# Token mixtures as scaling and addition, two more kinds of work given a choice of engine, and a first unit in halves

## The chip, the cores and the metric

The kernel runs on one core of one Trainium2 chip. Its metric is the device time of one execution in microseconds. Three runs of the kernel before gave 168.01 (median), 167.43 and 169.7 us. A core has a matrix engine (PE; its weight loads are shown apart, as PEld), a vector engine (DVE), a scalar engine (ACT), a general engine (POOL) and a queue that issues most transfers (SP). Each of them runs its own list of instructions strictly in order and waits on semaphores for the others.

## The reference, cut to what matters

Attention over a window of 128 tokens plus the first 4 tokens of the sequence, for 4 sequences of 768 tokens, 8 heads of 64 columns; then, on the 512 columns that the heads give together, a feed-forward part whose inputs are mixed from each token and the one before it.

```python
keep = is_sink | in_window            # 4 first tokens, or 0 <= pos_q - pos_k < 128
scores = np.where(keep, scale * q @ k.T, -1e9)
a = softmax(scores)
x = heads_side_by_side(a @ v)         # (4, 768, 512)

x_prev = concat([zeros, x[:, :-1]])
xk = mu_k * x + (1.0 - mu_k) * x_prev
xr = mu_r * x + (1.0 - mu_r) * x_prev
k = np.maximum(xk @ w_k, 0.0)         # 512 -> 1024
v = k * k @ w_v                       # 1024 -> 512
r = 1.0 / (1.0 + np.exp(-(xr @ w_r)))
out = r * v
```

## The kernel before, in words

**Units.** The 3072 tokens are 12 units of 256 (three to a sequence). A unit u goes through four stages: `prepare` (casts of k, q, v from float32 to bf16 into kb, qb, vb, and transposes of kb and qb into kt and qt, by PE and a copy, or by a transposing transfer), `attend` (per pair of heads: scores into two PSUM banks, exponential on ACT into e, multiplication of e by a mask on DVE, product with the values, reciprocal of the sums, and x, the scaled result), `mix` (transpose of x into xt, where a column is a token; td = xt minus xt shifted by one token; xk and xr) and `ffn` (keys: xk times wk into PSUM; rl = max(0, keys); kk = rl squared; gate: xr times wr, then th = tanh; product: kk times wv; ob = (th + 1) times product; store).

**The mixtures.** mu x + (1 - mu) x_prev is computed as td mu + x_prev. Line 973 does both steps in one DVE instruction (scalar_tensor_tensor), on 256 tokens of one of four groups of 128 columns: eight instructions in a unit, 96 in all.

**Squares and values.** The square (L1047) is a DVE multiplication of rl by itself, 48 times, 512 columns each. The scaling of the attention result (L911) is a DVE multiplication of a PSUM bank by the reciprocal, 48 times, 256 columns each.

**Choice and order.** Every operation is recorded with its engine (`P.op`), what it reads and writes, and the buffers that it takes from and holds in pools. Some have alternatives (`alts`); the table `CHOICE` says by number which one is built: the relu (L1035 on ACT, L1039 on DVE), the casts (L648 to L655, L714), the copies out of PSUM (L695, L700, L944), the casts of the weights (L609 to L615). `ORDER` holds a list of operations for each engine, written out by hand or by a search ahead of time; the planner walks these lists with assumed costs, only to give every operation its buffer and to place a few warming matmuls (L1098, L1101) in PE's early gaps. What runs on an engine, and in which order, is thus fixed by the two tables. A list that is late somewhere holds up all that stands behind it.

**The first unit.** Its k and q are loaded in two halves by heads (L455): heads 0 to 3 of all 256 tokens, then heads 4 to 7. Its keys need xk of all four groups of columns and all 256 tokens.

**Transfers.** All loads, the transposing transfers (L669, L955) and the stores (L1090, L1010) are issued by SP, except two small loads of mu by ACT. The weights come in five pieces of 1 MB (L473): two of wk, one of wr, two of wv. Outputs leave from ob, which has three buffers. The last 128 tokens are stored in two parts (L1010), of 128 and 384 columns, both by SP.

Of the kernel before, what the change touches and what calls it, by code (L numbers as in the profile page):

```python
# [18 lines left out]
    79: "POOL", 80: "POOL", 81: "POOL", 84: "ACT", 87: "ACT", 89: "DVE", 92: "DVE",  # L19
    94: "DVE", 95: "DVE", 97: "DVE", 98: "DVE", 131: "DVE", 134: "POOL", 137: "POOL",  # L20
    140: "ACT", 141: "DVE", 159: "PE/full", 171: "PE/tiles", 182: "POOL", 185: "POOL",
    187: "DVE", 191: "DVE", 195: "DVE", 241: "PE/tiles", 253: "PE/full", 264: "POOL",
    270: "POOL", 273: "DVE", 276: "ACT", 289: "DVE", 345: "POOL", 348: "POOL", 351:
    "DVE", 354: "POOL", 357: "ACT", 404: "PE/full", 416: "PE/tiles", 429: "POOL", 432:
    "POOL", 434: "POOL", 437: "DVE", 438: "ACT", 447: "DVE", 484: "PE/tiles", 496:
    "PE/full", 514: "POOL", 517: "ACT", 586: "POOL", 588: "POOL", 591: "POOL", 596:
    "ACT", 643: "PE/tiles", 655: "PE/full", 666: "POOL", 668: "POOL", 675: "ACT", 721:
    "PE/tiles", 733: "PE/tiles", 744: "POOL", 746: "POOL", 748: "POOL", 752: "ACT",
    753: "ACT", 819: "POOL", 821: "POOL", 823: "POOL", 828: "DVE", 847: "DVE", 872:
    "PE/tiles", 884: "PE/full", 897: "POOL", 901: "POOL", 904: "ACT", 923: "DVE", 948:  # L30
    "PE/tiles", 960: "PE/full", 979: "DVE", 1015: "DVE", 1019: "DVE",
# [19 lines left out]

OCT = range(1, 12)
# [282 lines left out]
def kernel(  # L335
# [14 lines left out]
    nc = tc.nc  # L350
# [807 lines left out]
```

## Time and profile before

| what | value |
|---|---|
| three runs, median (lowest, highest) | 168.01 us (167.43, 169.7) |
| the profiled execution's own time | 168.08 us |
| its span in the profile | 166.4 us |
| granted TensorE clock | 0.997 |
| PE busy | 155.0 us, 93% |
| DVE busy | 149.9 us, 90% |
| ACT busy | 116.6 us, 70% |
| POOL busy | 35.4 us, 21% |
| transfers | 34.38 MB, packets take 88.0% of the 16 engines' span |

The span runs from the first to the last instruction of the profiled execution; the execution's own time is 1.68 us longer. Busy time is a union: where instructions overlap, or the next begins before the end of the one before is recorded, nothing is counted twice. An instruction's duration is therefore longer than the distance at which a row of the same instructions starts; for sums on a full engine the distance from start to start counts, and that is what the chain of work and the timeline give. A PE that is busy in the profile may still wait a little between two matmuls, since their ends are modelled.

### The profile page before, as it was taken

The numbers are of one execution on the slowest core, as the hardware profiler recorded it, in microseconds if no ns is written. First come the engines' busy times: TensorE is split into PE (matmuls) and PEld (weight loads), VectorE is DVE, ScalarE is ACT, GpSimd is POOL, SyncE is SP. The second block draws the span as 40 slices with busy tenths as digits, with TensorE's granted clock in tenths as the row PEclk, the third lists the DMA queues.
The fourth block names the chain that finished last, engine by engine and source line by source line (L and its number), as shares of the span: only waits on it lengthen the run. The fifth ranks groups of instructions, "written<-read, shape, count | busy, mean of one in ns | idle before, by whom it ended". The sixth has DMA issues, their size and how long they took to land.

```text
span 166.4 us, 4712 instructions
## 1 busy us (share of the span) xinstructions
PE 155.0 (93%) x1858; PEld 102.4 (62%) x1858; DVE 149.9 (90%) x385; ACT 116.6 (70%) x190; POOL 35.4 (21%) x68
## 2 busy tenths in 40 slices
PE   7978678999999999999999999999998999999992
PEld 3545455665668586667567786485654664767541
DVE  7479999999899999999999999999979989995931
ACT  3388957996799999997978997783781647244111
POOL 2983332003606022134030060210210100000000
PEclk9999999999999999999999999999999999999998
DMA  4999999999898999999799999998995973301033
GB/s 133 253 373 389 241 260 328 387 360 325 198 290 230 229 246 248 195 226 197 173 234 138 161 206 197 219 207 109 209 174 113 246 199 126 121 9 63 0 132 120
DMA packets 74453, 34.38 MB, mean 207 GB/s; under 512 B 63800, under 2 KB 66112, under 8 KB 74432
## 3 DMA queue, kind: packets, MB, share of 16 engines
q1 hardware_dynamic: 74416, 34.09, 88.0%
q8 instruction: 14, 0.23, 0.6%
q14 instruction: 7, 0.06, 0.1%
q10 hardware_dynamic: 16, 0.00, 0.0%
HBM read 24.12 MB, written 6.29 MB: 183 GB/s over the span
## 4 chain that ended last, share of the span: by engine, by line
PE 35%; DVE 32%; DMA 16%; SPq 9%; issue 3%; POOL 2%; DVEq 0%; POOLq 0%
PE bank L1074 12%; DMA ks<-in_k_dram 11%; PE bank L1025 10%; DVE e L875 6%; DVE xr L973 5%; PE bank L1056 5%; SPq L431 5%; DVE x L911 4%; DVE xk L973 4%; DVE ob L1083 4%; DVE kk L1047 3%; DVE td L962 3%; DMA xt<-x 3%; DMA out_dram<-ob 3%; PE bank L681 2%
## 5 line engine op out<-in xcount | busy, mean ns | idle before, releaser
L1025 PE MATMUL bank<-xk,wk_sb 128*128 128x256 bf16 x384 | 50.9, 273 | 1.7 <-ACT rl L1035 1.0
L861 ACT ACTIVATE e<-sc 128x1024 bf16<-128x1024 f32 (+1 forms) x48 | 45.0, 966 | 4.9 <-PE sc L789 4.7
L1074 PE MATMUL bank<-wv_h,kk 128*128 128x512 bf16 x184 | 46.5, 379 | 1.4 <-DVE ob L1083 1.4
L1025 PEld LDWEIGHTS <-wk_sb 128*128 128x128 bf16 x384 | 35.6, 98 | 11.2 <-DVE wk_sb L615 1.3
L1035 ACT ACTIVATE rl<-bank 128x512 bf16<-128x512 f32 x44 | 25.8, 612 | 14.5 <-PE bank L1025 9.7
L875 DVE TENSOR_TENSOR e<-e,mask 128x1024 bf16<-128x1024 bf16 (+1 forms) x48 | 30.7, 654 | 0.3 <-ACT e L861 0.3
L1074 PEld LDWEIGHTS <-kk 128*128 128x128 bf16 x184 | 16.8, 97 | 16.3 <-issue 2.2
L1056 PE MATMUL bank<-wr_sb,xr 128*128 128x512 bf16 x96 | 24.5, 379 | 0.1
L973 DVE SCALAR_TENSOR_TENSOR xr<-td,mu_all,xt 128x256 bf16<-128x256 bf16 x48 | 24.4, 516 | 0.0
L1062 ACT ACTIVATE th<-bank 128x512 f32<-128x512 f32 x24 | 14.5, 609 | 10.9 <-PE bank L1056 9.6
L973 DVE SCALAR_TENSOR_TENSOR xk<-td,mu_all,xt 128x256 bf16<-128x256 bf16 x48 | 21.7, 479 | 0.1
L1047 DVE TENSOR_TENSOR kk<-rl 128x512 bf16<-128x512 bf16 x48 | 19.5, 425 | 0.3 <-ACT rl L1035 0.3
L911 DVE TENSOR_TENSOR x<-bank,rec 128x256 bf16<-128x256 f32 x48 | 19.4, 414 | 0.2
L1083 DVE SCALAR_TENSOR_TENSOR ob<-th,bank 128x512 f32<-128x512 f32 x23 | 15.7, 682 | 4.3 <-PE bank L1074 2.4
L894 PEld LDWEIGHTS <-e 128*128 128x128 bf16 x352 | 14.3, 97 | 3.6 <-DVE e L875 0.5
L894 PE MATMUL bank<-vb,e 128*128 128x65 bf16 x352 | 16.1, 193 | 0.3 <-ACT xt L944 0.3
L789 PE MATMUL sc<-qt,kt 64*64 64x128 bf16 (+4 forms) x496 | 12.8, 226 | 1.7 <-ACT e L861 0.9
L1056 PEld LDWEIGHTS <-xr 128*128 128x128 bf16 x96 | 8.9, 98 | 7.6
L789 PEld LDWEIGHTS <-kt 64*64 64x64 bf16 (+1 forms) x496 | 9.2, 106 | 5.7 <-issue 3.9
L714 POOL CAST vb<-vs 128x512 bf16<-128x512 f32 x10 | 7.0, 701 | 25.4 <-DMA vs<-in_v_dram 15.8
L962 DVE TENSOR_TENSOR td<-xt 128x512 bf16<-128x512 bf16 x24 | 11.6, 489 | 0.9 <-DMA xt<-x 0.7
L944 ACT COPY xt<-bank 128x512 bf16<-128x512 bf16 x15 | 8.8, 585 | 3.5 <-PE bank L935 3.0
(84 smaller groups left out, 151.9 us busy)
## 6 DMA issues: line engine op xcount, KB each, us to landing
vs<-in_v_dram SPq DMA_DIRECT2D x24, 256.0 KB, 5.7
out_dram<-ob SPq DMA_DIRECT2D x23, 256.0 KB, 3.0
ks<-in_k_dram SPq DMA_DIRECT2D x16, 256.0 KB, 4.4
qs<-in_q_dram SPq DMA_DIRECT2D x7, 512.0 KB, 5.9
qs<-in_q_dram SPq DMA_DIRECT2D x10, 256.0 KB, 5.1
ks<-in_k_dram SPq DMA_DIRECT2D x4, 512.0 KB, 9.4
w<-in_moe_w_k_dram SPq DMA_DIRECT2D x2, 1024.0 KB, 7.8
w<-in_moe_w_v_dram SPq DMA_DIRECT2D x2, 1024.0 KB, 11.0
```

Of the source, the lines that this page charges most:

```text
L789: nc.tensor.matmul(out=sc[keys, a, o0 + f0 - q0:o0 + f1 - q0], lhsT=lhs[rows, keys], rhs=qs[rows, f0:f1], start=u not in BIAS, stop=True, ...
L861: nc.scalar.activation(out=buf[ek][:, :, lo:], in_=buf[sck][:, :, lo:], func=AF.Exp, scale=scale)
L875: nc.vector.tensor_tensor(out=at, in0=at, in1=m, op=ALU.mult)
L894: nc.tensor.matmul(out=o[:, g, a, :], lhsT=e[:, a, e0:e0 + 128], rhs=rhs, start=(T == 0 and i == 0), stop=(i == len(blocks) - 1), skip_gro ...
L911: P.op("DVE", dve(256), lambda ok=ok, rk=rk, c=c: nc.vector.tensor_tensor(out=buf["x", u][:, :, 128 * c:128 * c + 128].rearrange("p g (a d ...
L973: nc.vector.scalar_tensor_tensor(out=buf[key][:, c, :], in0=buf[tk][:, i, :], scalar=mu[w][:, c:c + 1], in1=xt[:, c, t0 - 1:t0 + 255], op0 ...
L1025: nc.tensor.matmul(out=ps[:, i, :], lhsT=wk_sb[:, c, 128 * f:128 * f + 128], rhs=xk[:, c, :], start=(c == 0), stop=(c == NC - 1), skip_gro ...
L1035: nc.scalar.activation(out=buf[rk], in_=buf[psk].rearrange("p (i t) -> p i t", i=2), func=AF.Relu)
L1047: P.op("DVE", dve(512, 0.52), lambda f2=f2, rk=rk: nc.vector.tensor_tensor(out=buf["kk", u][:, 2 * f2:2 * f2 + 2, :], in0=buf[rk], in1=buf ...
L1056: nc.tensor.matmul(out=buf[psk], lhsT=buf["xr", u][:, c, 128 * g:128 * g + 128], rhs=wr_sb[:, c, :], start=(c == 0), stop=(c == NC - 1))
L1074: nc.tensor.matmul(out=buf[psk], rhs=wv_h[:, f, :], lhsT=buf["kk", u][:, f, 128 * g:128 * g + 128], start=(f == 0), stop=(f == NF - 1))
L1083: P.op("DVE", dve(512), lambda psk=psk, tk=tk, bk=bk: nc.vector.scalar_tensor_tensor(out=buf[bk], in0=buf[tk], scalar=1.0, in1=buf[psk], o ...
```

## The change

Four things, and then new tables.

1. **Mixtures in two steps, in all units** (`ADDED`, function `added`): xm = td mu, by two DVE instructions (tensor_scalar) or two ACT instructions (activation with a scale for each partition) of 256 columns, then xk or xr = xm + x_prev, one DVE addition of 512 columns. The buffer xm is new (four of them).
2. **Squares and value scalings may go to ACT.** On ACT a square is one activation of 512 columns; a scaling is four activations of 64 columns, one for each reciprocal.
3. **The first unit in halves of 128 tokens** (`load_first`, `attend_first`, `mix_first`, `keys_first`). k and q are loaded by halves of tokens, all heads. Scores, exponentials, masks, values, transposes, mixtures, keys, relus and squares work on the first 128 tokens and then on the next; the keys are 64 matmuls of 128 columns in place of 32 of 256, the masks 4 pairs of instructions in place of 4.
4. **The last store's smaller part** is issued by ACT in place of SP.

`CHOICE` and `ORDER` are new throughout. As the two programs are built, the engines' lists differ in these counts (first unit included):

| operation | before | after |
|---|---|---|
| DVE mixture, one step, 256 columns | 96 | 0 |
| DVE addition, 512 columns | 0 | 48 |
| scaling xm: DVE / ACT, 256 columns | 0 / 0 | 66 / 22 |
| scaling xm, first unit: DVE / ACT, 128 columns | 0 / 0 | 4 / 12 |
| square: DVE / ACT | 48 / 0 | 24 / 24 |
| value scaling: DVE / ACT (four instructions each) | 48 / 0 | 29 / 19 |
| relu: DVE / ACT | 4 / 44 | 13 / 35 |
| xt copied out of PSUM: DVE / ACT | 3 / 15 | 9 / 9 |
| kt, qt copied out of PSUM: DVE / ACT | 3 / 23 | 7 / 19 |
| cast of v: DVE / ACT / POOL | 4 / 10 / 10 | 10 / 4 / 10 |
| casts of k, q: DVE / ACT / POOL | 8 / 14 / 26 | 16 / 8 / 24 |
| casts of weights: DVE / ACT / POOL | 5 / 2 / 3 | 6 / 3 / 1 |

On SP the second piece of wk, which stood right behind the first, now stands behind v of unit 1 and k of unit 2; stores and loads of later units change places too. On PE the order of stages is much the same: attention of unit 1 ahead of the first keys, keys of unit 1 ahead of the products of unit 0.

```diff
...
+FIRST = 0
+
+ADDED = range(12)
...
+    pool("xm", 4, [128, 2, 256], BF16)
...
+    def load_first(u, g, rank):
+        for name, src in (("k", k), ("q", q)):
+            key = (name, u)
+            P.op("SP", 530.0, lambda key=key, src=src: nc.sync.dma_start(
+                out=quarters(buf[key], g).rearrange("p h j d -> p h (j d)"),
+                in_=src[0, :, 128 * g:128 * g + 128, :].rearrange(
+                    "(i h) (p j) d -> p i h (j d)", j=4, h=2)), rank, service=800.0,
...
-            load(0, "kq", -100, 0, 4)
-            load(0, "kq", -99.5, 4, 8)
+            for g in range(2):
+                load_first(FIRST, g, -100 + g / 2)
...
+    def attend_first(u, rank):
...
+        for g in range(2):
+            for cp in range(2):
+                r = rank + 2 * g + cp
+                tile = cp + 1 if g else 0
+                sk, ek, ok, rk = [(n, u, i) for n, i in (
+                    ("sc", tile), ("e", tile), ("o", 2 * g + cp), ("rec", 2 * g + cp))]
+                new = g or not cp
...
+                width = 1024 if g else 512
...
+                def scaled(g=g, cp=cp, ok=ok, rk=rk, view=view):
+                    for i in range(2):
+                        for a in range(2):
+                            x0 = 256 * cp + 128 * i + 64 * a
+                            nc.scalar.activation(
+                                out=buf["x", u][:, g, x0:x0 + 64], in_=view(ok)[:, i, a, 0:D],
+                                func=AF.Copy, scale=buf[rk][:, i, a, :])
...
+    def mix_first(u, rank):
+        xt, t0 = xts[0], 16
+        for g in range(2):
...
+                def scaled_dve(w=w, tk=tk, mk=mk):
+                    for c in range(NC):
+                        nc.vector.tensor_scalar_mul(out=flat(mk)[:, c, :], in0=flat(tk)[:, c, :],
+                                                    scalar1=mu[w][:, c:c + 1])
...
+                P.op("DVE", dve(512, 0.52), lambda g=g, s0=s0, key=key, mk=mk: (
+                    nc.vector.tensor_tensor(
+                        out=buf[key][:, :, 128 * g:128 * g + 128], in0=flat(mk),
...
+    def keys_first(u, rank):
+        for g in range(2):
+            for f4 in range(2):
+                psk, rk, r = ("kp", u, g, f4), ("rl", u, g, f4), rank + 2 * g + f4
...
+                    def keys(half=half, f4=f4, psk=psk, ts=ts):
+                        ps = buf[psk].rearrange("p (i t) -> p i t", i=4)
+                        for i in range(2 * half, 2 * half + 2):
+                            f = 4 * f4 + i
+                            for c in range(NC):
+                                nc.tensor.matmul(out=ps[:, i, :],
+                                                 lhsT=wk_sb[:, c, 128 * f:128 * f + 128],
+                                                 rhs=buf["xk", u][:, c, ts], start=(c == 0),
+                                                 stop=(c == NC - 1), skip_group_check=True)
...
+                def square(f4=f4, rk=rk, ts=ts):
+                    nc.scalar.activation(out=buf["kk", u][:, 4 * f4:4 * f4 + 4, ts],
+                                         in_=four(buf[rk]), func=AF.Square)
+
+                def square_dve(f4=f4, rk=rk, ts=ts):
+                    nc.vector.tensor_tensor(out=buf["kk", u][:, 4 * f4:4 * f4 + 4, ts],
+                                            in0=four(buf[rk]), in1=four(buf[rk]), op=ALU.mult)
...
     def attend(u, rank):
+        if u == FIRST:
+            attend_first(u, rank)
+            return
...
+            def scaled(ok=ok, rk=rk, c=c):
+                for g in range(2):
+                    for a in range(2):
+                        nc.scalar.activation(
+                            out=buf["x", u][:, g, 128 * c + 64 * a:128 * c + 64 * a + 64],
+                            in_=view(ok)[:, g, a, 0:D], func=AF.Copy,
+                            scale=buf[rk][:, g, a, :])
+
+            P.op("DVE", dve(256), scaled_dve, r + 1, take=[] if k else [("x", ("x", u))],
+                 alts={"DVE": (dve(256), scaled_dve, False),
+                       "ACT": (560.0, scaled, False)},
...
+    def added(u, half, w, key, tk, xt, t0, rank, reads):
+        mk = ("xm", u, half, w)
+        c0 = 2 * half
+
+        def scaled_dve():
+            for i in range(2):
+                nc.vector.tensor_scalar_mul(
+                    out=buf[mk][:, i, :], in0=buf[tk][:, i, :], scalar1=mu[w][:, c0 + i:c0 + i + 1])
+
+        def scaled():
+            for i in range(2):
+                nc.scalar.activation(out=buf[mk][:, i, :], in_=buf[tk][:, i, :], func=AF.Copy,
+                                     scale=mu[w][:, c0 + i:c0 + i + 1])
+
+        P.op("DVE", 2 * dve(256, 0.26), scaled_dve, rank, port=True,
+             alts={"DVE": (2 * dve(256, 0.26), scaled_dve, True),
+                   "ACT": (2 * act(256), scaled, False)},
+             take=[("xm", mk)], hold=[tk], reads=[tk, ("mu", w)], writes=[mk])
+        P.op("DVE", dve(512, 0.52), lambda: nc.vector.tensor_tensor(
+            out=buf[key][:, c0:c0 + 2, :], in0=buf[mk], in1=xt[:, c0:c0 + 2, t0 - 1:t0 + 255],
+            op=ALU.add), rank, port=True, take=[] if half else [(key[0], key)],
+            hold=[mk] + ([key] if half else []),
+            reads=[mk] + reads + ([key + (0,)] if half else []),
+            writes=[key + (2 * half,), key + (2 * half + 1,)])
...
+                if u in ADDED:
+                    added(u, half, w, key, tk, xt, t0, r + 4 * w, made + prev)
+                    continue
...
-            P.op("SP", 400.0, lambda bk=bk, cols=cols, n=n: nc.sync.dma_start(
-                out=out[B - 1, S - 128:S, cols], in_=buf[bk][:, 0:n]), rank, hold=[bk],
-                reads=[bk], service=1.5 * n + 20.0)
+            queue = nc.sync if part else nc.scalar
+            P.op("SP" if part else "ACT", 400.0, lambda bk=bk, cols=cols, n=n, queue=queue: (
+                queue.dma_start(out=out[B - 1, S - 128:S, cols], in_=buf[bk][:, 0:n])), rank,
+                hold=[bk], reads=[bk], service=1.5 * n + 20.0)
...
+            def square(f2=f2, rk=rk):
+                nc.scalar.activation(out=buf["kk", u][:, 2 * f2:2 * f2 + 2, :], in_=buf[rk],
+                                     func=AF.Square)
...
+            P.op("DVE", dve(512, 0.52), square_dve, rank + f2, port=True,
+                 alts={"DVE": (dve(512, 0.52), square_dve, True),
+                       "ACT": (act(512), square, False)},
...
```

More of the change, by code (lines that the diff above doesn't have):

```diff
@@ L18 @@
 CHOICE = {
[L19 to L30, printed above, removed]
@@ L32 @@
+    982: "ACT", 992: "DVE", 993: "ACT", 997: "ACT", 1020: "DVE", 1021: "ACT", 1024:
+    "DVE", 1025: "ACT", 1028: "DVE",
 }
@@ L645, in cast @@
             def cast(copy, raw=raw, rk=rk, hs=hs, half=half, name=name):
+                if u == FIRST:
+                    js = slice(4 * half, 4 * half + 4)
+                    return lambda: copy(
+                        out=eights(buf[rk])[:, js].rearrange("p j h d -> p h j d"),
+                        in_=quarters(buf[raw], half))
                 if octet(name, u):
@@ L693, in evacuate @@
             def evacuate(copy, half=half, psk=psk, key=key, name=name):
+                if u == FIRST:
+                    return lambda: copy(
+                        out=buf[key][:, :, half, :].rearrange("p c (t j) -> p c t j", j=4),
+                        in_=buf[psk].bitcast(BF16)[:, 0:512].rearrange(
+                            "p (j t c) -> p c t j", j=4, c=NP))
                 if octet(name, u):
@@ L920, in mix @@
     def mix(u, rank):
+        if u == FIRST:
+            mix_first(u, rank)
+            return
         b, T = divmod(u, NT)
```

193 lines of the change are left out of this document (178 added, 15 removed), and 141 rows, old and new, of the table ORDER.

## The prediction

> **What bounds it now.** I read the page's first two parts, then the chain that ended last in order of time, then PE's, DVE's and ACT's timelines.
>
> ```profile
> span 166.4 us, 4712 instructions
> ...
> PE 155.0 (93%) x1858; PEld 102.4 (62%) x1858; DVE 149.9 (90%) x385; ACT 116.6 (70%) x190; POOL 35.4 (21%) x68
> ...
> PE   7978678999999999999999999999998999999992
> ...
> DVE  7479999999899999999999999999979989995931
> ACT  3388957996799999997978997783781647244111
> ...
> PEclk9999999999999999999999999999999999999998
> ```
>
> PE is full from slice 8 (29 us), DVE from slice 4 but for a few digits to slice 36, and ACT nearly so from slice 8 to 19 (80 us). A full digit does not say which of them sets the pace, so I count work. The chain, a start and a length on each line, gives the distances from start to start that the sums need:
>
> ```profile
> 40.10 0.49 PE bank L894 x16
> ...
> 48.11 0.45 PE sc L789 x16
> ...
> 57.52 0.45 PE bank L681 x8
> ...
> 72.62 1.20 DVE e L875 x2
> ...
> 82.23 1.14 DVE xk L973 x3
> ...
> 126.23 0.34 DVE td L962
> ...
> 137.57 0.61 DVE ob L1083
> ...
> 150.94 3.49 PE bank L1025 x32
> ...
> 154.44 4.32 PE bank L1074 x20
> 158.75 0.86 PE bank L1056 x4
> ...
> 162.00 0.66 PE bank L995 x4
> ```
>
> **PE's work:** 384 keys at 3.49/32 = 0.109 us (41.9), 184 products at 0.216 (39.7), 96 gates at 0.215 (20.7), 352 value matmuls at 0.031 (10.8), 24 score operations at 0.45 (10.8), 176 transposes at 0.056 (9.9), the last product 1.8, sink parts some 5.3: 141 us, without warming matmuls. PE ends at 162.66 (the last line), so 21.7 us of it are not work. Where are they? One line of PE's timeline splits them:
>
> ```profile
> 34.78 0.60 PE L1025 MATMUL bank<-xk,wk_sb 128*128 128x256 bf16 x4
> ```
>
> This is the last key work of unit 1; it is over at 34.78 + 4 x 0.109 = 35.2. By PE's list 18.4 us of work lie up to there, so **16.8 us** are lost at the start, and only 162.66 - 35.2 - (141 - 18.4) = **4.9 us** in the 127 us after it. The remaining 166.4 - 162.66 = **3.7 us** are the tail. DVE's work counted in the same way is 141.9 us (busy 149.9, the difference being overlap and interference with POOL), ACT's 109.5. So PE is the floor, DVE stands right beside it, and an easier DVE can return at most the 4.9 us.
>
> **The change, part by part.**
>
> *DVE.* Mixtures: 96 one-step instructions at 0.40 (1.14/3 = 0.38 at best) leave, 38.4. 48 additions come, with the form of td: 0.335 each, 16.1. The 66 scalings of 256 columns have no row. Bounds: the reciprocal of 4 elements, 0.10 from start to start, and td, 0.34. The nearest form is the cast of 512 float32 columns (L655, L714), 0.335, whose 256-column half would be some 0.20 if 0.07 of it is fixed; bf16 halves the bytes, so I take 0.15: 9.9, and 0.4 for the first unit's four. By the Trainium skill, "VectorE: DVE Perf Modes", section on the perf-mode tier table, a bf16 tensor_scalar in SBUF runs at four elements a cycle, from which an estimate is 0.07 + 0.07 = 0.14; no run here shows it. Mixtures: -12.0 (bounds -15 to 0). Squares: 24 x 0.335 = -8.0. Value scalings: 19 x 0.335 = -6.4. Back come 9 relus at 0.60, 6 copies of xt and 6 casts of v and 8 of k, q at 0.335, 4 copies of kt, qt and a weight cast at 0.60: +15.1. The first unit's masks add 0.3. Sum -11.0: DVE 141.9 to 131.
>
> *ACT.* Its distances:
>
> ```profile
> 104.25 0.59 ACT L1035 ACTIVATE rl<-bank 128x512 bf16<-128x512 f32 x1
> 104.72 0.82 ACT L861 ACTIVATE e<-sc 128x768 bf16<-128x768 f32 x1
> ...
> 117.84 0.38 ACT L765 ACTIVATE es<-bank 128x256 bf16<-128x256 f32 x1
> 118.11 1.95 ACT L861 ACTIVATE e<-sc 128x1024 bf16<-128x1024 f32 x2
> ```
>
> 512 columns take 0.47 to 0.49, 256 take 0.27, so 64 take 0.11 to 0.15 on that line, and I take 0.13 (bounds 0.08, by the two-column activation at the start, and 0.27). New: 24 squares 11.8, 76 pieces of 64 columns 9.9, 22 scalings of 256 columns 5.9 to 6.2, twelve of 128 columns 2.0. Gone: 9 relus, 6 + 4 PSUM copies, 6 casts of v, 6 of k, q at about 0.49 to 0.52, less one weight cast: -14.6. Net +15.8: 109.5 to 125.3, still below PE.
>
> Here a rule speaks against the change. The Trainium skill, "VectorE: DVE Perf Modes", section "The TRN2 errata", gives ScalarE 172 cycles plus one a column from PSUM and 224 plus one a column from SBUF at 1.2 GHz: an estimate of 0.197 us for 64 columns and 0.40 for 256 from SBUF. As starts this adds some 12 us more to ACT. The row of es agrees with it as a length (0.38 against 0.357) and not as a distance (0.27), so I stay with 0.13.
>
> *PE.* 64 keys of 128 columns at 0.056 (as transposes) for 32 at 0.109: +0.1. The rest is the same within 0.2: 141.
>
> *Start.* The halves help only if what stands behind them is early. k and q of the first 128 tokens are as many bytes as four heads were, so they land alike (4.7 us for k). DVE's list has the copies of the second half's kt and qt ahead of the first mask, and that half's k is cast on POOL behind the masks that it makes; the first mask comes at about 9.3 (8.93 before). ACT then has two 1024-column exponentials, a cast and a copy ahead of its half of the first x, which is scaled by some 13.1; transpose and copy bring the first td to 14.0 (14.24 before). The first piece of wk is waited for until 16.04 by POOL; as much is loaded ahead of it as before, so keys cannot start before about 17.2 (18.44 before). The second piece has 1 MB more ahead of it (v of unit 1, k of unit 2): at the 241 to 387 GB/s of these slices 2.7 to 4.3 us, so it lands near 23 to 24, where DVE and ACT reach its casts at about 22.5; behind DVE's cast wait x and td of unit 1. Up to xk of unit 1 DVE has 23.2 us of work (22.1 before), and that came at 28.9; with the same 6.8 us of idle time it would be 30.0, with the 0.9 us less that the earlier first td leaves, 29.1. I take 29.4. PE has done 12.9 us of its list by then (12.1 before, at 28.82): a loss of 16.5 in place of 16.7. So the start gives 0.3: 16.5, bounds 14 (keys of the first half fill the gap from 17 to 23) and 19 (the second wk piece and ACT both late).
>
> *Middle.* DVE drops to 93% of PE's work; ACT rises to 89%, most of it before 75 us, where it had least room. 4.9 falls to 3.0, bounds 1.5 and 6.
>
> *Tail.* One of SP's two last issues (0.81 for both) goes to ACT, where nothing stands behind it: 3.7 to 3.3; at worst 3.7.
>
> **Sum:** 16.5 + 141 + 3.0 + 3.3 = 163.8. The execution took 168.08 for a span of 166.4, 1.7 around it: **165.4 us**, against its own 168.08, which is the median of the runs within 0.1.
>
> **Rivals.**
> 1. *The halves do pay at the start.* PE's digits 7, 8, 6, 7 and 8 in slices 3 to 7 leave some 5.8 us open between 8 and 29 us; if first-half keys and values fill half of them and unit 1 comes earlier by as much, the loss is 13.5: **162.4**. Against it stand the landing of wk and a DVE that is full from 14 to 29 us in either kernel.
> 2. *ACT becomes the bound early, slower than before.* By the end of unit 2's exponentials (35.8 us: 33.96 and 1.95) ACT had 24.7 us of work and 11.1 idle; it will have 29.9. From the point where less than 5.2 of those 11.1 us can be filled, the exponentials come late, and x, xk and PE's keys of unit 2 with them. If none can, +5.2 without DVE's gain: **173**; with half of them, 170.5. The Trainium skill's section on the errata would, by the estimate above, bring ACT near 137 and so to this case. For it: ACT is idle at the start because it waits for PE and transfers, which more work on ACT does not fill. Against: 6 of the 11 us lie after 7.6 us, between its own waits.
> 3. *Nothing changes.* SP issues without a pause from 60 to 133.8 us, and DVE waited for xt by transfer until 136.8 and for a store of ob until 124.78. If the transfers set the pace of units 7 to 10, PE's and DVE's room is given back as waits there: **168**.
>
> **Chances.** Forecast 0.50, first rival 0.25, second 0.13, third 0.12. Two per cent of 168.01 (164.65, 171.4) is about what a measurement can tell. Of the forecast's half, spread over 163.5 to 167.5, 0.15 lies below 164.65; with 0.21 of the first rival, faster is 0.36. Slower is 0.08, most of the second rival beyond its half-way price. The range takes in the first rival but its best part, and the second up to its middle: 161.8 to 169.8.
>
> **What would show it.** In the changed kernel's profile: DVE busy near 138 and ACT near 132; the scalings at 0.10 to 0.20 from start to start; the last key work of unit 1 over at 34.5 to 36; PE's digits at 9 from slice 8 on, and PE's end near 160.4. I am wrong if unit 1's keys start before 27 (first rival), or if ACT's digits are 9 from slice 3 to 12 while PE's fall below (second).

## The result, and the profile after

The changed kernel takes 173.78 us (median of four, 173.54 to 175.09), the kernel before 168.42 beside it: a ratio of 1.033, interval 1.024 to 1.042. It is **slower**; forecast were 165.4 us and a range to 169.8. The profiled execution took 173.62 us for a span of 171.9. Here and below, medians and ranges in microseconds are of all executions of a run, while ratios and their intervals, always to the kernel before run beside it, leave out those more than 1.5% above the fastest of their kernel.

The page of the changed kernel: span, busy times, the rows of slices, and the shares of the chain that ended last.

```profile
span 171.9 us, 4887 instructions
...
PE 160.9 (94%) x1893; PEld 106.2 (62%) x1893; DVE 144.1 (84%) x402; ACT 140.7 (82%) x294; POOL 34.3 (20%) x64
...
PE   6887967999999999999999999999899999999991
...
DVE  6489977998998999899899999887699859785641
ACT  3369998999999989998999999968979868569211
...
PEclk9999996999999999999999999999999999999998
...
PE 54%; ACT 20%; DVE 16%; DMA 4%; issue 2%; POOL 1%; DVEq 0%; SPq 0%
```

DVE lost 5.8 us of busy time (149.9 before), ACT gained 24.1 (116.6 before). ACT's row is at 9 from slice 4 to slice 26 but for three digits of 8, while PE has 6 and 7 in slices 6 and 7. In the chain before, ACT was not among the shares shown; now it is the second, with 20%. In slice 7 the granted clock is 0.6. The shares of the chain before were these:

```profile
PE 35%; DVE 32%; DMA 16%; SPq 9%; issue 3%; POOL 2%; DVEq 0%; POOLq 0%
```

PE's timeline around the end of the start (start, length, engine, line, operation, tiles, shape, count, and in brackets the idle time before it and who ended it):

```profile
21.11 1.82 PE L948 MATMUL bank<-xk,wk_sb 128*128 128x128 bf16 x24
...
23.52 0.61 PE L948 MATMUL bank<-xk,wk_sb 128*128 128x128 bf16 x8
...
26.15 0.33 PE L1081 MATMUL bank<-vsink,es 128*128 128x130 bf16 x3 [1.52 <-ACT x L1170]
...
27.58 1.04 PE L948 MATMUL bank<-xk,wk_sb 128*128 128x128 bf16 x8 [0.58 <-ACT wk_sb L640]
...
38.18 0.60 PE L1321 MATMUL bank<-xk,wk_sb 128*128 128x256 bf16 x4
```

The same timeline of the kernel before begins its keys so:

```profile
18.44 0.50 PE L1025 MATMUL bank<-xk,wk_sb 128*128 128x256 bf16 x3
```

The first keys start at 21.11 (18.44 before). PE then waits 1.52 us for ScalarE's value scalings and 0.58 for a weight cast that stands behind them on ScalarE. The last key work of unit 1 is over at 38.18 + 0.44 = 38.62 (35.2 before).

What the first keys wait for shows in ACT's timeline of the changed kernel:

```profile
16.78 1.28 ACT L922 ACTIVATE xm<-td,mu_all 128x128 bf16<-128x128 bf16 x4
...
18.70 1.95 ACT L1110 ACTIVATE e<-sc 128x1024 bf16<-128x1024 f32 x2
20.51 2.45 ACT L922 ACTIVATE xm<-td,mu_all 128x128 bf16<-128x128 bf16 x8
...
25.13 0.96 ACT L1170 ACTIVATE x<-bank,rec 128x64 bf16<-128x64 f32 x4
...
41.31 1.07 ACT L1110 ACTIVATE e<-sc 128x1024 bf16<-128x1024 f32 x1
```

The last line is the last exponential of unit 2; it is over at 42.4, against 35.9 before. VectorE's queue holds the keys as well: their second group needs the columns of wk that it casts behind the mixtures of the first half, until 20.99:

```profile
20.31 0.68 DVE L646 CAST wk_sb<-w 128x1024 bf16<-128x1024 f32 x1
```

The distances from start to start, in the chain in order of time:

```profile
20.80 2.16 ACT xm L922 x7
...
87.69 0.82 ACT x L1170 x4
...
107.38 0.79 ACT xm L1193 x2
...
118.91 0.87 DVE xm L1188 x4
...
143.22 0.52 ACT kk L1344
...
167.54 0.66 PE bank L1288 x4
```

In these rows a value piece of 64 columns costs ScalarE 0.82/4 = 0.205 us, a scaling of 256 columns 0.395, one of 128 columns 0.31, a square 0.52. Over all pairs of such instructions in the trace with no idle time between them, the medians from start to start are 0.197, 0.40, 0.29 and 0.52. PE ends at 168.20. By the split of the prediction, about 18.1 of PE's 140.9 us of work (as counted there) lie ahead of 38.62, so **20.5 us** are lost at the start (16.8 before), 168.20 - 38.62 - 122.8 = **6.8** in the middle (4.9 before), and the tail is 171.9 - 168.2 = **3.7**, as before. Start +3.7 and middle +1.9 are the whole difference of the spans (5.5 us).

### The profile page after: what moved, and what is told of

Its sections match the earlier page's. It is cut to its first block, busy times and chain, and to the rows that moved or that the text cites. A ratio compares the mean times of both kernels' runs of the same rounds, so it can differ in the third digit from the quotient of the medians.

```text
span 171.9 us, 4887 instructions
## 1 busy us (share of the span) xinstructions
PE 160.9 (94%) x1893; PEld 106.2 (62%) x1893; DVE 144.1 (84%) x402; ACT 140.7 (82%) x294; POOL 34.3 (20%) x64
## 4 chain that ended last, share of the span: by engine, by line
PE 54%; ACT 20%; DVE 16%; DMA 4%; issue 2%; POOL 1%; DVEq 0%; SPq 0%
PE bank L1379 15%; PE bank L1321 14%; PE bank L1360 7%; ACT e L1110 6%; DMA xt<-x 4%; PE bank L717 3%; PE bank L1143 3%; DVE xm L1188 3%; ACT x L1170 3%; PE sc L1036 3%; DVE e L1124 2%; ACT rl L1331 2%; ACT xm L922 2%; PE bank L1225 2%; ACT kk L1344 2%
## 5 line engine op out<-in xcount | busy, mean ns | idle before, releaser
L1321 PE MATMUL bank<-xk,wk_sb 128*128 128x256 bf16 x352 | 46.0, 273 | 0.5 <-DVE xk L1200 0.2
L1110 ACT ACTIVATE e<-sc 128x1024 bf16<-128x1024 f32 (+1 forms) x44 | 42.3, 989 | 2.2 <-PE sc L1036 2.2
L1331 ACT ACTIVATE rl<-bank 128x512 bf16<-128x512 f32 x31 | 18.6, 614 | 5.5 <-PE bank L1321 5.3
L1170 ACT ACTIVATE x<-bank,rec 128x64 bf16<-128x64 f32 x72 | 17.1, 347 | 1.2 <-DVE rec L1157 1.0
L1344 ACT ACTIVATE kk<-rl 128x512 bf16<-128x512 bf16 x24 | 15.3, 649 | 2.5 <-DVE rl L1335 2.5
L1143 PE MATMUL bank<-vb,e 128*128 128x65 bf16 x328 | 15.3, 193 | 0.9 <-DVE vsink L782 0.5
L755 POOL CAST vb<-vs 128x512 bf16<-128x512 f32 x10 | 7.4, 740 | 41.8 <-DMA vs<-in_v_dram 41.7
L1188 DVE TENSOR_SCALAR xm<-td,mu_all 128x256 bf16<-128x256 bf16 x66 | 15.6, 287 | 0.1
L688 POOL CAST kb<-ks 128x512 bf16<-128x512 f32 x9 | 8.1, 899 | 22.6 <-DMA ks<-in_k_dram 12.5
L1335 DVE TENSOR_SCALAR rl<-bank 128x512 bf16<-128x512 f32 x13 | 8.8, 685 | 4.4 <-PE bank L1321 4.4
L1036 PE MATMUL sc<-qt,kt 64*64 64x128 bf16 (+2 forms) x480 | 12.1, 226 | 0.0
L1193 ACT ACTIVATE xm<-td,mu_all 128x256 bf16<-128x256 bf16 x22 | 10.1, 534 | 1.8 <-DVE td L1252 1.6
```

What stands on the lines that cost most here:

```text
L1036: nc.tensor.matmul(out=sc[keys, a, o0 + f0 - q0:o0 + f1 - q0], lhsT=lhs[rows, keys], rhs=qs[rows, f0:f1], start=u not in BIAS, stop=True, ...
L1110: nc.scalar.activation(out=buf[ek][:, :, lo:], in_=buf[sck][:, :, lo:], func=AF.Exp, scale=scale)
L1143: nc.tensor.matmul(out=o[:, g, a, :], lhsT=e[:, a, e0:e0 + 128], rhs=rhs, start=(T == 0 and i == 0), stop=(i == len(blocks) - 1), skip_gro ...
L1170: nc.scalar.activation(out=buf["x", u][:, g, 128 * c + 64 * a:128 * c + 64 * a + 64], in_=view(ok)[:, g, a, 0:D], func=AF.Copy, scale=buf[ ...
L1188: nc.vector.tensor_scalar_mul(out=buf[mk][:, i, :], in0=buf[tk][:, i, :], scalar1=mu[w][:, c0 + i:c0 + i + 1])
L1321: nc.tensor.matmul(out=ps[:, i, :], lhsT=wk_sb[:, c, 128 * f:128 * f + 128], rhs=xk[:, c, :], start=(c == 0), stop=(c == NC - 1), skip_gro ...
```

## The experiments

Two theories at first. **A:** ScalarE's small instructions cost more than summed, and ScalarE became the bound. **B:** the start's lists, halves and landings are late by themselves. There are two more: **C** (TensorE's half clock near 27 us) and **D** (VectorE's price of the mixtures). Busy times are of each run's profile; "unit 1" is when the last key work of unit 1 is over in it, "unit 8" when the last key matmul of unit 8 starts (left out for act_cheap, whose profiled execution, 174.98 us, was the longest of its four). Each profile is one execution. How far two of them can differ shows in squares_late: it moves nothing ahead of 115 us, yet its key matmuls of units 7 and 8 come 1.5 us later than before.

| run | ratio to before (interval) | DVE | ACT | unit 1 | unit 8 |
|---|---|---|---|---|---|
| before | 1 | 149.9 | 116.6 | 35.2 | 120.4 |
| changed | 1.033 (1.024-1.042) | 144.1 | 140.7 | 38.6 | 126.9 |
| act_cheap | 1.015 (1.005-1.025) | 146.3 | 128.9 | - | - |
| dve_cheap | 1.029 (1.022-1.036) | 133.0 | 140.4 | 37.6 | 126.1 |
| both_cheap | 1.010 (1.006-1.014) | 131.7 | 128.3 | 35.3 | 121.2 |
| warm_fill | 1.030 (1.019-1.041) | 145.5 | 140.5 | 38.0 | 125.7 |
| start_lists | 1.038 (1.030-1.046) | 145.7 | 140.5 | 38.2 | 127.3 |
| mix_only | 1.040 (1.032-1.049) | 156.2 | 117.0 | 38.4 | 127.7 |
| mix_spaced | 1.017 (1.008-1.026) | 150.2 | 116.8 | 36.3 | 123.3 |
| squares_act | 1.009 (1.004-1.013) | 142.7 | 127.9 | 35.3 | 124.1 |
| squares_late | 1.002 (0.998-1.006) | 148.2 | 121.1 | 35.3 | 121.9 |
| values_act | 1.020 (1.012-1.028) | 144.9 | 130.3 | 35.0 | 123.7 |
| start_changed | 1.029 (1.018-1.039) | 152.5 | 122.5 | 40.0 | 126.1 |
| halves_only | 1.046 (1.038-1.054) | 156.8 | 117.3 | 41.7 | 128.8 |
| halves_lists | 1.042 (1.031-1.054) | 155.4 | 117.1 | 41.2 | 127.6 |
| rest_changed | 1.022 (1.015-1.030) | 145.0 | 135.6 | 35.4 | 124.2 |
| rest_cheap2 | 1.014 (1.004-1.023) | 143.8 | 127.2 | 36.7 | 123.4 |
| fused_again | none | 152.4 | 133.5 | 38.5 | 128.6 |

### The two sums brought to what the prediction took

act_cheap:

```diff
-for g in range(2):
-    for a in range(2):
-        nc.scalar.activation(x[g, 64 columns], scale=rec[g, a])
+nc.scalar.activation(x[256 columns], scale=0.01)
-for i in range(2):
-    nc.scalar.activation(xm[:, i, :], td[:, i, :], scale=mu[c0 + i])
+nc.scalar.activation(xm, td, scale=mu[c0])
```

> The changed kernel with its lists untouched; ScalarE's scalings are each one instruction over the whole tile with one constant scale (values: one of 256 columns in place of four of 64; mixtures: one of 512 in place of two of 256 or four of 128), so the per-head division and the per-channel factors are left out there. By the rows ScalarE then loses 19 x (0.88 - 0.33) + 11 x (0.78 - 0.49) + 3 x (1.23 - 0.49) = 16 us and comes to 125, the sum that the prediction took. Theory A (the price of ScalarE's small instructions is what was lost): 167 to 169, ScalarE's share of the chain of waits falls from 20% to under 8%, no 1.5 us stall of PE at 24.4. Theory B (the first unit's lists and landings are what was lost): 172 to 173.5. Theory C (only TensorE's half clock from 27 to 30.5 us): the stall at 24.4 goes and the clock with it, 171 to 172.

Measured: 171.63 (170.03 to 174.98), ACT busy 128.9. This lies between A and B, and the number alone fits C too (171 to 172), which warm_fill tests below. Of the 3.3% lost, ScalarE's price is about half (1.033 to 1.015, with intervals of 0.9 and 1.0% to either side), and 1.5% stays. The edit also takes away ScalarE's wait for the reciprocals.

dve_cheap, and both edits together in both_cheap:

```diff
-for i in range(2):
-    nc.vector.tensor_scalar_mul(xm[:, i, :], td[:, i, :], mu[c0 + i])
-nc.vector.tensor_tensor(xk, xm, xt, op=ALU.add)
+nc.vector.tensor_tensor(xk, td, xt, op=ALU.add)   # where VectorE scaled
```

> The changed kernel with its lists untouched and the 70 scalings on VectorE left out (the additions read the difference itself, so these mixtures aren't scaled); ScalarE's stay. VectorE loses 66 x 0.20 + 4 x 0.3 = 14 us and comes to about 131, the sum that the prediction took; ScalarE stays near 141. Theory A (ScalarE alone holds the pace): under 1 us gained, 173 to 174. Theory D (VectorE's mixtures, at 0.85 us for a pair in place of the 0.635 taken, hold the pace in the middle): unit 8's keys come 2 to 3 us earlier than 126.9, time 170 to 171.5.

> The scalings of the run above left out and ScalarE's scalings as in the run with one instruction for each: VectorE near 131 and ScalarE near 125, the two sums that the prediction took, with the changed kernel's lists and its halved first unit. If the two sums were the whole mistake (A and D): 164.5 to 167. If the lists, the halves and the landings cost something of their own (B): 168 to 171, and then the loss should stand ahead of unit 1's keys, which end at 35.1 in the kernel before.

Measured: 173.38 with VectorE's scalings gone, 170.97 with both. VectorE alone gives back next to nothing: theory A's number, and against D. With both sums even lower than predicted (DVE 131.7, ACT 128.3 on the page, against near 138 and 132 forecast) PE's start and middle are, in the profiled execution, those of the kernel before. The page, and the last key work of unit 1 in PE's timeline, of both_cheap:

```profile
span 166.9 us, 4739 instructions
...
PE 157.0 (94%) x1893; PEld 104.3 (62%) x1893; DVE 131.7 (79%) x332; ACT 128.3 (77%) x217; POOL 31.5 (19%) x64
```

```profile
34.91 0.60 PE L1314 MATMUL bank<-xk,wk_sb 128*128 128x256 bf16 x4
```

It is over at 35.35, 0.15 behind the kernel before, with the first unit in halves and, over the whole span, 18 us less on VectorE. So in this execution the late start is not transfers, and the halves don't shorten it either: what the two engines have to do ahead of unit 1's keys sets it, and below that amount something else does. It is the fastest of the run's ten, 168.74 us at a mean granted clock of 1.0; the others took 169.73 to 172.23 at 0.977 to 0.999, and no profile shows where those lost the rest of the 1.0%. The forecast of 165.4 would not have come even at its own prices.

### The clock and the start's lists

warm_fill:

```diff
-for i in range(2 * half, 2 * half + 2):            # unit 0, second half, second group of keys
+for i in list(range(2 * half, 2 * half + 2)) * 4:
```

> The changed kernel with eight matmuls of unit 0's last but two key group issued four times over (the same results, some 1.4 us more TensorE work) ahead of the place where TensorE waits from 24.4 to 26.15 us for ScalarE's value scalings. Nothing else moves. Theory C: TensorE is no longer idle in the stretch before 27.15, the granted clock stays at 1.0 through 27 to 31 us (mean clock of the span 0.997 in place of 0.986), and the work that ran at half pace there comes 1 to 1.7 us earlier: 172 to 172.8. Theory A: the clock may stay, but ScalarE is what keeps the pace there, so under 0.5 us: 173.3 to 174.

Stretches of the changed kernel, then of warm_fill (the stretch, its length, busy time and count on PE, weight loads, DVE, ACT and POOL, granted clock, share of DMA, GB/s):

```profile
23.70:27.10 3.40, 1.50 (x28) 1.09 (x25) 3.19 (x9) 3.40 (x9) 0.00 (x0) 1.00 1.11 352
27.20:30.50 3.30, 2.92 (x28) 2.92 (x29) 2.25 (x7) 2.81 (x9) 0.00 (x0) 0.50 1.12 346
```

```profile
23.70:27.10 3.40, 2.77 (x56) 2.52 (x52) 3.07 (x9) 3.40 (x9) 0.00 (x0) 1.00 1.10 344
27.20:30.50 3.30, 2.72 (x46) 2.60 (x47) 2.54 (x9) 3.30 (x9) 0.00 (x0) 1.00 1.11 347
```

Where PE was busy for 1.50 of 3.40 us, the next 3.3 us ran at half the clock; with the added matmuls (2.77) they did not. So the mechanism of C is there, but by unit 1's keys it is worth 38.62 - 38.04 = 0.6 us, and the time (median 174.15) doesn't resolve it: with the clock kept, ScalarE is full in both stretches (3.40 of 3.40 and 3.30 of 3.30).

start_lists:

```diff
 POOL: -hmask, ident, sinks, ...            +ident, hmask, sinks, ...
 PE:   -mup, q half 0, k half 0, k half 1, first scores
       +q half 0, k half 0, first scores, mup, k half 1
```

> The changed kernel with three places of its lists at the start set back to the order of before: on GpSimd the identity ahead of the head mask, on PE the transpose of the mixture factors and the second quarter's key transposes behind the first scores. Theory B: PE's warming isn't broken at 4.06 us, full speed from about 5 and not 10 us, first scores at 7.2 in place of 8.15, and a time of 171.5 to 173. Theory A: ScalarE and the landings set what follows, the gain is lost by the time of unit 1's keys: 173.3 to 174.

Measured: 175.04, no gain. The first scores, the clock's rise and unit 1's keys (38.16) come earlier (6.98 in place of 8.15, 5.86 in place of 10.08, 0.5 us), the first two as B says, and nothing of it is left at the end, as A says.

### One part of the change at a time, on the kernel before

> The kernel before with one part of the change alone: each pair of fused mixtures becomes two VectorE scalings of 256 columns and one addition of 512; engines, first unit and every list stay as before, the pair standing where the first of its two mixtures stood. By the prediction's price (a scaling 0.15 us) a pair costs 0.30 + 0.335 against 0.80, so 48 pairs take 8 us off VectorE: busy near 142, time 164 to 166.5. By the price read from the trace after (about 0.205) a pair costs 0.745 against 0.80: VectorE loses only 2.6, time 167 to 168.5, no difference that can be measured. Slower than 169 would mean that the intermediate tile adds waits of its own.

```diff
-for i in range(2):
-    nc.vector.scalar_tensor_tensor(xk[c0 + i], td[:, i, :], mu[c0 + i], xt[c0 + i])
+for i in range(2):
+    nc.vector.tensor_scalar_mul(xm[:, i, :], td[:, i, :], mu[c0 + i])
+nc.vector.tensor_tensor(xk[c0:c0 + 2], xm, xt[c0:c0 + 2], op=ALU.add)
```

Measured: 175.31, 6.7 us slower, and outside what either price allowed: by the expectation, the intermediate tile adds waits of its own. VectorE's timeline of mix_only:

```profile
91.84 0.48 DVE L1166 TENSOR_SCALAR xm<-td,mu_all 128x256 bf16<-128x256 bf16 x2
92.35 0.43 DVE L1178 TENSOR_TENSOR xr<-xm,xt 128x512 bf16<-128x512 bf16 x1
92.69 0.48 DVE L1166 TENSOR_SCALAR xm<-td,mu_all 128x256 bf16<-128x256 bf16 x2
```

From the first scaling to the next pair it is 0.85 us, against 0.79 for two fused mixtures. The two scalings end at 92.32 and the addition starts at 92.35: it doesn't overlap the instruction whose tile it reads, as the second scaling overlaps the first. Over the 48 pairs the median from the second scaling to the addition is 0.316 us, from scaling to scaling 0.196. To test it, each addition is put one instruction later, with nothing else changed:

```diff
 DVE: -xm(half), add(half), next, ...
      +xm(half), next, add(half), ...
```

> The kernel before with mixtures as scaling and addition on VectorE, as in the first run of this study (175.3), but each addition one VectorE instruction later, so that it isn't right behind the scaling that it reads. If the wait of the addition for the scaling (0.316 us from start to start in place of 0.196) is what made that run slow, 48 x 0.12 = 5.8 us of VectorE go: busy near 150, time 169 to 171. If the scalings' number itself or GpSimd's port is the reason: 173 to 175.

The same view of mix_spaced:

```profile
90.77 0.41 DVE L1178 TENSOR_TENSOR xk<-xm,xt 128x512 bf16<-128x512 bf16 x1
91.11 0.47 DVE L1166 TENSOR_SCALAR xm<-td,mu_all 128x256 bf16<-128x256 bf16 x2
91.50 0.68 DVE L1102 TENSOR_TENSOR e<-e,mask 128x1024 bf16<-128x1024 bf16 x1
```

Two scalings now take 0.39 and an addition 0.34: 0.73. VectorE's busy time falls from 156.2 to 150.2, the time from 175.31 to 170.04. Eleven of its additions still stand right behind a scaling, but one of another pair, and they start 0.196 after it: what costs 0.12 is reading the tile just written, not the change of operation. This wait is shown as the main part of mix_only's loss. A further 1.7% (0.8 to 2.6) remain, with VectorE as busy as before (150.2 against 149.9), and no run shows their cause.

squares_act, squares_late and values_act move operations from VectorE's list to ScalarE's (24 squares; the 8 of units 8 to 11; 18 value scalings in four pieces each):

```diff
-DVE: kk(u, f)                              +ACT: kk(u, f)
-DVE: x(u, k) in one instruction            +ACT: x(u, k) in four of 64 columns
```

> The kernel before with one part of the change alone: the same 24 squares are on ScalarE (each at the place in ScalarE's list that its time on VectorE gives); mixtures fused, value scalings on VectorE, first unit whole, all other lists as before. VectorE loses 24 x 0.335 = 8 us (149.9 to 142), ScalarE gains 24 x 0.52 = 12.5 (116.6 to 129). Theory D (VectorE is what PE waits for in the kernel before): 163.5 to 166.5. Theory A (ScalarE has no room between 40 and 100 us, where it is busy for 18 of 20): 168 to 171, with exponentials and PE's scores late behind squares.

> The kernel before with eight squares on ScalarE alone, those of units 8 to 11, where ScalarE is busy for 12 of 20 us and VectorE for 16 to 18. VectorE loses 2.7 us, ScalarE gains 4.2, none of it ahead of 115 us. Theory A: no cost there, 167.5 to 168.7, and up to 0.8 us of PE's waiting for VectorE from 120 to 150 us is won (167.5). If ScalarE's exponentials are late there too: 169 to 170.

> The kernel before with one part of the change alone: the 18 value scalings of units 1 to 11 that the change puts on ScalarE stand there as four instructions of 64 columns each, all else as before. VectorE loses 18 x 0.335 = 6.0 us, ScalarE gains 72 x 0.205 = 14.8 (116.6 to 131). Theory A (ScalarE has no room from 10 to 100 us): 170.5 to 173, more than the squares cost, since more of them stand ahead of 100 us and each holds ScalarE longer. Theory D (VectorE is what PE waits for): 165 to 167.

Measured: 169.96, 168.68 and 171.4. Each frees VectorE (by 7.2, 1.7 and 5.0 us) and none is faster; each also loads ScalarE. The start isn't touched; the last key matmul of unit 8 comes 3.7 us later with the squares and 3.2 with the value scalings, of which 1.5 can be the difference between two profiles. Theory A fits where ScalarE was busy for 18 of 20 us; in units 8 to 11, where it had room (11.6 of 20 before from 120 to 140 us), the squares cost nothing that shows, and win nothing.

fused_again undoes the mixtures of units 1 to 11 in the changed kernel:

```diff
-ADDED = range(12)
+ADDED = ()
```

> The changed kernel with the mixtures of units 1 to 11 fused again on VectorE, standing where the additions stood (unit 0, squares, value scalings and lists as changed). VectorE: 88 x 0.397 = 34.9 in place of 66 x 0.20 + 44 x 0.335 + 12 x 0.12 = 29.4, so plus 5.5; ScalarE minus 22 x 0.39 = 8.6. Theory D: VectorE holds the pace, 176 to 179. Theory A: ScalarE holds it, 171 to 173. If both count alike: 173 to 175.

Measured: 175.5, 175.78, 178.15 and 179.37 (no interval), VectorE busy 152.4, ScalarE 133.5. The two shorter ones are 1.7 and 2.0 us above the changed kernel's median, between D's number and that of "both count alike"; A's is missed. It points to the split helping in this kernel, though alone it hurts: only four of the changed kernel's 48 additions start 0.31 to 0.32 us behind a scaling, and 22 scalings are on ScalarE. Without an interval that is not shown.

### The start against the rest

start_changed takes the changed lists for the first 34 us of the plan and those of before after it; rest_changed the reverse.

```diff
 start_changed: FIRST = 0, ADDED = (); each list: [changed, planned before 34 us] + [rest as before]
 rest_changed:  FIRST = -1, ADDED = range(1, 12); each list: [before, planned before 34 us] + [rest as changed]
```

> The kernel before with the start of the changed one: the first unit in halves and the changed lists and engines up to about unit 1's keys (some 35 us), from there on the lists and engines of before, with fused mixtures for units 1 to 11, squares and value scalings on VectorE, the last stores on SP's queue. Theory B (the changed start costs 3.3 us by the time of unit 1's keys, and what is behind it costs the rest): unit 1's keys end near 38.0 to 38.5, time 171 to 172. If nothing is lost in the start that isn't won back: 168 to 169.

> The other half: the first unit whole and the lists and engines of before up to about unit 1's keys, from there on the changed lists with mixtures as scaling and addition, 22 squares and 16 value scalings on ScalarE. Theory A (ScalarE's price is lost wherever ScalarE is full): unit 1's keys end near 35.1 as before, unit 8's 2 to 3 us later than the 120.4 of before, time 170 to 171.5. If the loss behind the start was only carried on from it: 168 to 169.

Measured: 173.46 and 171.73, ratios 1.029 and 1.022. Either part alone makes the kernel slower. They sum to more than the whole (5.1% against 3.3%), so it seems that the losses overlap; the joint of two lists made apart may cost something too. In start_changed unit 1's keys end at 40.0, later than in the changed kernel (38.6) and than expected (38.0 to 38.5), with the mixtures of unit 1 fused on VectorE there.

What makes the start late? halves_only takes all scalings of it off ScalarE; halves_lists also sets four places of its lists back.

```diff
-P.op("ACT", xm(0, g, w)); add: xk = xm + xt          # 3 of 4
+add: 4 x nc.vector.scalar_tensor_tensor(xk[c], td[c], mu[c], xt[c])   # 128 columns each
-ACT: x(0, 0, 1), x(1, 0), x(1, 3) in four pieces     +DVE: one instruction each
 halves_lists also: POOL ident ahead of hmask; PE mup and k half 1 behind the first scores;
                    SP second piece of wk behind the first
```

> The kernel with the changed start (the run before), with the scalings of that start taken off ScalarE: unit 0's mixtures are fused on VectorE again (four of 128 columns each), and the three value scalings of units 0 and 1 that stood on ScalarE are one VectorE instruction each. What is left of the change is the first unit in halves with the changed lists of the first 35 us. Theory A (ScalarE's small instructions make the start late): unit 1's keys end at 35.5 to 37 in place of 39.9, time 168.5 to 170.5. Theory B (halves, lists and landings make it late): 38 or later, 171.5 to 173.

> The run above with four places of the start's lists set back to the order of before: on GpSimd the identity ahead of the head mask, on PE the mixture factors' transpose and the second quarter's key transposes behind the first scores, on SP the second piece of the key weights right behind the first. Theory B: a further 1 to 2 us, and if the halves pay at all, this is the kernel that shows it: unit 1's keys at 34.5 to 36, time 166.5 to 169. Theory A: no more than 0.5 us against the run above.

Measured: 175.06 and 174.4. A is missed, B's time too (its sign, unit 1's keys at 38 or later, came), and the start became **later**. PE's timeline of halves_only, and two of its stretches in the form above:

```profile
27.93 0.66 PE L1132 MATMUL bank<-vb,e 128*128 128x65 bf16 x16 [2.31 <-DVE e L1113]
...
41.27 0.60 PE L1310 MATMUL bank<-xk,wk_sb 128*128 128x256 bf16 x4
```

```profile
15.80:19.10 3.30, 3.30 (x47) 2.75 (x45) 3.30 (x7) 2.65 (x5) 1.69 (x2) 0.50 1.00 192
29.50:32.80 3.30, 3.10 (x30) 3.10 (x31) 3.17 (x10) 2.40 (x4) 0.00 (x0) 0.50 1.11 323
```

PE waits 2.31 us for a mask of unit 1 that stands behind the added work on VectorE: there, work taken off ScalarE is late on VectorE. But the clock is a rival here. PE ran at half of it in both stretches, the kernel before in neither; each lasted 3.41 us, so by estimate up to 2 x 1.7 us of the 6.5 by which unit 1's keys are late can be its, and no run parts the two. The lists are worth 0.5 us by unit 1's keys (41.21 against 41.71). Theory B falls as far as these four places of the lists go; what the halves as such cost the start is open, but they aren't free: four one-step mixtures of 128 columns take 1.06 us on VectorE there, so the unit's sixteen take 4.2, against 3.2 for eight of 256.

rest_cheap and rest_cheap2 (one kernel) ask whether the rest's loss is ScalarE's price: rest_changed with the edit of act_cheap.

> The kernel with the start of before and the rest changed (171.7), with ScalarE's scalings one instruction each with one constant scale (per-head division and per-channel factors left out there, as in the earlier run). ScalarE loses 16 x 0.5 + 11 x 0.25 = 11 us. Theory A: the 3.6 us that the changed rest cost are ScalarE's price, so 168 to 169.5. If it is the changed lists or the additions' waits on VectorE: 170.5 to 171.7.

> The run before once more, with more rounds, since its four executions lay between 168.1 and 173.1 and gave no interval. Theory A (ScalarE's price is what the changed rest costs): a ratio to the kernel before under 1.010, against 1.022 of the run with ScalarE's full price. If the changed lists and the additions' waits cost it: 1.015 to 1.022.

Measured: 170.97 (168.13 to 173.06, no interval), then 172.15, ratio 1.014 (1.004 to 1.023): between the two expectations, so this stays open. In the second run's profile it is 57.5 us from unit 1's last key matmul to unit 5's, against 59.0 in rest_changed, and 65.0 against 64.2 from there to unit 11's: what ScalarE's lower price gave up to unit 5 was partly lost again, with PE's longest waits behind unit 1 spread over ScalarE, VectorE and a transfer of kt (0.3 to 0.6 us each). These differences are no larger than the 1.5 us by which two profiles can differ. And its start, with the lists of before, came 1.3 us later than rest_changed's (36.7 against 35.4): 0.9 ahead of its first keys (19.30 against 18.44), the rest behind a stretch at half clock:

```profile
20.80:24.00 3.20, 3.20 (x17) 2.09 (x16) 3.20 (x7) 2.37 (x4) 0.00 (x0) 0.50 0.85 220
```

## Why the prediction was wrong

Two steps failed above all: ScalarE's prices, and with them the path of the start, which was led over VectorE and the landing of wk and in fact ran through ScalarE's queue as well.

- *ACT's price: wrong, and a main cause.* 0.13 for 64 columns, 0.27 to 0.28 for 256 and 0.17 for 128 measured 0.205, 0.395 and 0.31 in the chain: 76 x 0.075 + 22 x 0.12 + 12 x 0.14 = 10 us more (9 by the medians), and 0.7 for the squares. Busy came to 140.7, not 132. (The prediction's own terms add to 15.3, not to its 15.8; that is small beside it.) The step that failed was to draw a line through distances of other shapes (es, 256 columns from PSUM) down to 64 columns and over to a source in SBUF. The rule set aside there, the Trainium skill's "VectorE: DVE Perf Modes", section "The TRN2 errata", gives by estimate 0.197, 0.40 and, for 128 columns from SBUF, 0.29: the medians here are just these, so for these three it holds as a distance from start to start. For the longer square of 512 columns its estimate of 0.61 does not (0.52), nor for es (0.27 against 0.357). The experiments give this term about half of the loss (1.033 to 1.015).
- *The second rival named this mechanism.* ACT is at 9 from slice 4 on, PE falls to 6 and 7, unit 2's exponentials end 6.5 us late, and its upper price was 173, with 173.8 measured. It had 0.13. That its number came so close is in part luck: ScalarE's price accounts for about half of the loss. Its counter-argument, that ScalarE's idle time at the start could be filled, is what the wait of 1.52 us at 24.6 and the late unit 1 speak against.
- *DVE: the instruction mis-sized, the wait missed.* A scaling took 0.196, not 0.15, within the bounds; the estimate of 0.14 from the Trainium skill's "VectorE: DVE Perf Modes", section on the perf-mode tier table, does not hold here. No bound had the 0.12 us of an addition right behind its scaling. Busy fell by 5.8, not 11. In the changed kernel this hardly counts (dve_cheap, 1.029); in the mixtures alone it is most of 6.7 us.
- *"An easier DVE can return" some of the 4.9 us, and the halves 0.3: wrong.* both_cheap has both sums below the forecast and is 1.0% slower than before. VectorE freed by squares_act or values_act returned nothing either, though both load ScalarE. Less on VectorE than in the kernel before returned nothing in any run, while more on it did cost: mix_only added 6.3 us of busy time and lost 6.7.
- *Start:* predicted 16.5, measured 20.5, beyond the bound of 19. The first keys came at 21.11, not from 17.2: on PE's list scores of unit 1 stand ahead of them and wait for ScalarE's exponentials (18.70), which stand behind four scalings of unit 0 (16.78). The landing of wk (17.28 on POOL) had been watched, that queue not, nor VectorE's cast of the columns that the second group of keys needs (over at 20.99). That the halves cost nothing on the engines fails with halves_only, where they cost VectorE 1 us in unit 0's mixtures alone, though the clock may have a part in that run's late start.
- *Clock:* not in the sum at all; 0.6 us by unit 1's keys.
- *Middle:* 6.8 instead of 3.0, beyond the bound of 6; rest_changed shows a loss there without the changed start. How much of it is ScalarE's price and how much lists and transfers was not settled.
- *Tail:* 3.7, the bound "at worst"; the second issue queue gained nothing that shows.
- *PE's work* (141 us) was taken over for the split above, not measured anew. The third rival's reading that room given on VectorE comes back as waits fits the runs; that transfers set the pace was not tested. With both prices as forecast the ratio of 1.010 lies between its 168 and the second rival's half-way 170.5.

## What to carry to other kernels

Price a split instruction by its own kind, source and width, from start to start: the fixed part does not shrink with the columns, so four pieces of 64 columns cost 0.79 to 0.82 us, while one of 256 from PSUM goes by in 0.27 (es). Before moving work from a full engine to one that is 70% busy, look at the second's share in the stretch where the work falls: at 18 of 20 us ScalarE took nothing without loss here. Read the granted clock of every run before comparing its start with another's. And put something between an instruction and the one that reads its tile on the same engine.

## What was not expected of the hardware

- VectorE overlaps an instruction with the next by about 0.085 us, unless the next reads what it wrote: 0.316 in place of 0.196 us behind a 256-column scaling, 48 times; spaced by one instruction, 6.0 us of busy time and 5.3 of time went.
- A stretch of 3.4 us in which PE was busy for 1.50, with no idle time longer than 1.52, was followed by 3.41 us at half clock: eight 128-column matmuls took 1.04 us in place of 0.61. In dve_cheap it was so behind 2.13 us of 3.41, with no idle time over 0.6; behind warm_fill's 2.77 of 3.40 it was not.
- A store can hold VectorE for long: in warm_fill's profile it waited 3.1 us at once, until 138.2 us, for a store of ob to leave its buffer, in the changed kernel's 0.5 at most.
